# One row of a transposed activation: from four TensorE transposes to a transposing transfer, in a kernel whose instruction order is a table

## The chip, the cores and the metric

The kernel runs on one core of a Trainium2 chip. The metric is the time of one execution on the device in microseconds (us). Before the change the median of three executions was 614.86 us (614.82 to 615.6).

The engines of a core run side by side, each through its own queue in order: PE (TensorE, matrix products), DVE (VectorE), ACT (ScalarE), POOL (GpSimd) and SP (which here only issues transfers). An instruction that waits for a semaphore holds back everything behind it on its engine.

## The reference

One transformer block in float32 on 2048 rows of 512 numbers:

```
h  = x + A(layernorm(x))
h2 = h + B(layernorm(h))
A(x): q, k, v = x @ wqkv, 32 heads of 16; each position attends to 8 positions,
      itself and those 2, 4, ... 14 back; softmax; (attn @ v) @ wo
B(x): (gelu(x @ w_gate) * (x @ w_up)) @ w_down       with an inner width of 1792
```

What matters here is the seam between the two halves: B's products need layernorm(h) transposed, features on the partitions.

## The kernel before, in words

**Tiling.** The 2048 rows are four chunks (c = 0 to 3) of 512, each of four "rows" (j = 0 to 3): tiles of 128 positions on the partitions. Every float32 product is made as three products of rounded operands: a value is cut into a high part (copied on ACT, `split`, L412) and a low part (the rest, subtracted on DVE or POOL, L413), and PE adds high x high, high x low and low x high. So each tile that goes into a product appears as a pair, `hTh` and `hTl` for the transposed h.

**Stages.** Chunk by chunk: project to q, k and v (`project_pair`, with a scheme that shares products between two rows, L764; `project`, L501, for v), attention on DVE (`pk`, `lg`, `pv`), the output product `wo` (L501), then the feed-forward half in 14 steps (`pg`, `pu`, `acc`). Chunks 2 and 3 end together in `joint` and `last_sums`. The stages of different chunks overlap: while chunk 0 crosses the seam, PE still has products of chunk 3's projection to do (`qkc_3_0`, `qkc_3_1`, `qkv_3_2_...`).

**The seam, `tail(c)`, L939.** For each row j of a chunk: PE makes `wo_c_j` (12 products), DVE adds x to it (L968, into `h`), takes statistics (L478, L479), POOL makes the reciprocal deviation (L480, L481), DVE writes the normalised row `xhat_h` (L482). The row is then transposed in one of two ways. `transpose4` (L419): four PE transposes into one PSUM bank (L424), then the high part is copied by ACT and the low part subtracted by DVE from there. `crossed` (L451): ACT copies the row's 32-bit words into planes of 16-bit halves (L436), SP issues a transposing transfer back over the row (L438), ACT weaves the halves together again (L442), and the split follows. The table `CROSS_H` (L63) names the rows of each chunk that are crossed. The first product of the feed-forward half, `pg_0_0`, reads all four rows of `hTh_0`.

```
    def turn(src, flat, tmp, w=D, into=False):

        words = lambda t: t()[:, 0:w].bitcast(U16)
        planes, pairs = "p (h f) -> p h f", "p (f h) -> p h f"
        act(w * 1.65 + 100, lambda: nc.scalar.copy(words(tmp).rearrange(planes, h=2), words(flat).rearrange(pairs, h=2)),
            src, [(tmp, None)])
        plan.add("SP", 1330, lambda: nc.sync.dma_start_transpose(
            words(flat).rearrange("p (k t) -> p k t", t=P), words(tmp)), [(tmp, None)], src, nbytes=800 * w)
        if into:
            return
        act(w * 2.28 + 100, lambda: nc.scalar.copy(words(tmp).rearrange(pairs, h=2), words(flat).rearrange(planes, h=2)),
            src, [(tmp, None)])
...
        a = ring(n, 2, [P, D], name=f"a_{nm}", at=lambda k: slots[k])
        turn(src, flat, a, w)
        split(hi, lo, lambda: a()[:, 0:w].rearrange("p (k t) -> p k t", t=P), [(a, None)], wh, wl, size=w)
```

**Buffers in turn.** The normalised rows `xhat_h` have two buffers and so have the planes `a_h`: row 2 uses those of row 0, and row 3 the `xhat_h` buffer of row 1. A buffer is free again when its last reader is done. For `xhat_h` of a crossed row that is the second ACT copy (L442), for `a_h` the low part's subtraction (L413). The PSUM banks of `wo_0_j` alternate between two as well. The feed-forward weights come in as `fraw_0_f` (768 KB each, L1025); the buffer of `fraw_0_0` held chunk 3's sums `xS_3_1`, which the last products of `qkc_3_1` read.

**The order.** Nothing on the chip chooses an order. The program first lists about 2860 operations with their dependences; then `Plan.schedule` (L305) sorts them by a number each from the table `PLACES` (L64), and the table `SWAPS` (L220) names operations that go to their other engine (ACT or DVE, DVE or POOL). Every engine's queue is the sorted list, restricted to it.

## Time and profile before

| | |
|---|---|
| median of three executions | 614.86 us |
| the profiled execution | 615.18 us, of which span 613.1 us |
| instructions in the profile | 8418 |
| PE busy | 606.3 us (99%), 2692 matmuls and transposes |
| DVE busy | 523.4 us (85%) |
| ACT busy | 472.7 us (77%) |
| POOL busy | 364.3 us (59%) |
| granted TensorE clock | 0.999 |
| TensorE transposes of rows of h (`tp_h`) | 12, three rows of four |
| transposing transfers of rows of h | 13 |

The span reaches from the first to the last instruction; what is over in the execution's own time (2.1 us) lies around it. Matmuls are pipelined: one of 512 columns is listed with 389 ns, but the next one starts 227 to 228 ns later. In the lists below, rows of PE are therefore longer than their cadence.

### The profile page before, as it was taken

To read this page: it belongs to the slowest core of one execution; us is meant where nothing else is said; L and a number is where in the kernel's file an instruction comes from. 1 tells how busy PE (TensorE), PEld (TensorE's weight loads), DVE (VectorE), ACT (ScalarE), POOL (GpSimd) and SP (SyncE) were. 2 spreads that over 40 slices of the span, in tenths; PEclk is the share of its full clock that TensorE was granted. 3 is DMA by queue.
4 is the path that set the end of the run, shared out by engine and by line. 5 is a ranking of instruction groups with operands and counts; after the bars stand their busy time and mean duration, and the time that the engine had idled before them with its cause. 6 is when DMAs were issued, how large, how long until landed. Compare 5 with 4: busy or idle time off the path is not lost.

```text
span 613.1 us, 8418 instructions
## 1 busy us (share of the span) xinstructions
PE 606.3 (99%) x2692; PEld 498.8 (81%) x2692; DVE 523.4 (85%) x644; ACT 472.7 (77%) x822; POOL 364.3 (59%) x349
## 2 busy tenths in 40 slices
PE   8999999999999999999999999999999999999997
PEld 6778888888888888888888888888887888888886
DVE  6989999998999989999999979347977886779933
ACT  5998999748678879999779988768876656658850
POOL 4649898535899847695866944516324535422491
PEclk9999999999999999999999999999999999999999
DMA  8469888887999979999997979987479765557983
GB/s 301 140 231 257 266 238 253 257 276 220 316 333 336 296 239 295 305 284 309 375 353 239 289 227 208 298 267 221 114 246 231 236 215 190 203 190 209 253 259 103
DMA packets 110012, 154.50 MB, mean 252 GB/s; under 512 B 51456, under 2 KB 64512, under 8 KB 109584
## 3 DMA queue, kind: packets, MB, share of 16 engines
q1 hardware_dynamic: 109552, 153.57, 80.7%
q8 instruction: 21, 0.34, 0.2%
q10 hardware_dynamic: 416, 0.39, 0.2%
q14 instruction: 23, 0.19, 0.1%
HBM read 106.43 MB, written 36.23 MB: 233 GB/s over the span
## 4 chain that ended last, share of the span: by engine, by line
PE 95%; DMA 2%; DVE 1%; POOL 1%; issue 0%; ACT 0%; POOLq 0%
PE pg L501 12%; PE pu L501 12%; PE dn L1324 10%; PE pa L1206 8%; PE qkv L501 8%; PE wo L501 7%; PE qka L764 6%; PE pc L1206 5%; PE acc L1006 4%; PE acc L1005 4%; PE acc L1004 4%; PE qkc L764 3%; PE pu L1447 2%; PE pg L1447 2%; PE qkb L764 2%; DMA fraw<-in_wffn_dram 1%
## 5 line engine op out<-in xcount | busy, mean ns | idle before, releaser
L916 POOL TENSOR_TENSOR pv<-pv 128x1024 f32<-128x1024 f32 (+1 forms) x40 | 78.1, 1959 | 6.7 <-DVE pv L911 4.9
L911 DVE TENSOR_TENSOR pv<-vw,qp 128x2048 f32<-128x2048 f32 x32 | 72.2, 2281 | 5.3 <-ACT qp L891 4.4
L869 DVE TENSOR_TENSOR pk<-kw,qp 128x2048 f32<-128x2048 f32 x32 | 72.9, 2280 | 0.5 <-DMA kw<-kv 0.2
L872 DVE TENSOR_REDUCE lg<-pk 128x128 f32<-128x2048 f32 x32 | 72.7, 2279 | 0.1
L501 PE MATMUL pg<-hTh,gu 128*128 128x512 f32 x224 | 59.9, 389 | 0.0
L501 PE MATMUL pu<-hTh,gu 128*128 128x512 f32 x224 | 59.9, 389 | 0.0
L501 PEld LDWEIGHTS pg<-hTh,gu 128*128 128x128 f32 x224 | 42.0, 188 | 8.9 <-ACT hTh L412 0.2
L501 PEld LDWEIGHTS pu<-hTh,gu 128*128 128x128 f32 x224 | 42.0, 188 | 8.7
L1004 PE MATMUL acc<-dnh,gh 128*128 128x512 f32 x112 | 43.7, 390 | 0.0
L1006 PE MATMUL acc<-dnh,gl 128*128 128x512 f32 x112 | 43.6, 390 | 0.0
L1005 PE MATMUL acc<-dnl,gh 128*128 128x512 f32 x112 | 43.6, 389 | 0.0
L1236 ACT COPY jt<-pa 128x512 f32<-128x512 f32 x32 | 18.8, 586 | 25.8 <-PE pa L1206 15.2
L413 POOL TENSOR_TENSOR gu<-fraw,gu 128x512 fp32r<-128x512 f32 x25 | 32.5, 1309 | 7.2 <-ACT gu L412 7.2
L918 POOL TENSOR_TENSOR o<-pv 128x256 f32<-128x256 f32 x27 | 22.9, 854 | 16.8 <-DVE pv L916 11.3
L1206 PE MATMUL pa<-tt,jh 128*128 128x512 f32 x112 | 30.1, 391 | 0.1
L501 PE MATMUL pg<-hTl,gu 128*128 128x512 f32 x112 | 29.9, 389 | 0.0
L501 PE MATMUL pu<-hTl,gu 128*128 128x512 f32 x112 | 29.9, 389 | 0.0
L413 POOL TENSOR_TENSOR gl<-g,gh 128x512 fp32r<-128x512 f32 x21 | 27.2, 1299 | 3.9 <-ACT gh L412 3.9
L1206 PEld LDWEIGHTS pa<-tt,jh 128*128 128x128 f32 x112 | 20.9, 188 | 4.8 <-ACT jt L1236 0.5
L1006 PEld LDWEIGHTS acc<-dnh,gl 128*128 128x128 f32 x112 | 21.0, 188 | 4.5 <-DVE gl L413 0.2
L1005 PEld LDWEIGHTS acc<-dnl,gh 128*128 128x128 f32 x112 | 21.0, 188 | 4.4
L501 PEld LDWEIGHTS pg<-hTl,gu 128*128 128x128 f32 x112 | 21.0, 188 | 4.4
(512 smaller groups left out, 1841.8 us busy)
## 6 DMA issues: line engine op xcount, KB each, us to landing
fraw<-in_wffn_dram SPq DMA_DIRECT2D x47, 768.0 KB, 5.7
kw<-kv SPq DMA_DIRECT2D x16, 704.0 KB, 6.2
vw<-kv SPq DMA_DIRECT2D x16, 704.0 KB, 6.2
gu<-ld SPq DMA_DIRECT2D x19, 512.0 KB, 5.4
kv<-qkvt SPq DMA_DIRECT2D x32, 256.0 KB, 3.3
ld<-gu SPq DMA_DIRECT2D x14, 512.0 KB, 3.9
ws<-sums_kw SPq DMA_DIRECT2D x21, 256.0 KB, 2.3
x<-in_x_dram SPq DMA_DIRECT2D x16, 256.0 KB, 4.8
```

The lines of the kernel that those rows point to most:

```text
L413: sub = lambda eng: eng.tensor_tensor(lo(), src(), hi().bitcast(F32), op=ALU.subtract)
L501: nc.tensor.matmul(acc(), a, b, start=(p == k == 0 and not seeded), stop=(p == n - 1 and k == KD - 1), skip_group_check=seeded)
L764: nc.tensor.matmul(acc(), a(k), b()[:, k], start=first and q == k == 0, stop=q == 2 and k == 1, skip_group_check=not first)
L869: nc.vector.tensor_tensor(pr(), k4, q2.unsqueeze(2).to_broadcast([P, 2, W, QF]), op=ALU.mult)
L872: dve(2195, lambda pr=pr, jj=jj: nc.vector.tensor_reduce(lg()[:, i, jj:jj + 2], pr().rearrange("p j w (h d) -> p j w h d", d=DH), axis=AX. ...
L911: nc.vector.tensor_tensor(pr().rearrange("p j w (h d) -> p j w h d", d=DH), v5, e5, op=ALU.mult)
L916: either(home, 256 * m, lambda eng, pr=pr, m=m: eng.tensor_tensor(pr()[:, :, 0:m], pr()[:, :, 0:m], pr()[:, :, m:2 * m], op=ALU.add), [], ...
L1004: nc.tensor.matmul(a, gh()[:, sl], dh(), start=(i == 0 and not SEED), stop=False, skip_group_check=SEED)
L1005: nc.tensor.matmul(a, gh()[:, sl], dl(), start=False, stop=False, skip_group_check=SEED)
L1006: nc.tensor.matmul(a, gl()[:, sl], dh(), start=False, stop=(i == NF - 1), skip_group_check=SEED)
L1206: nc.tensor.matmul(acc(), a[:, k], b(k), start=first and p == k == 0, stop=p == 2 and k == 1, skip_group_check=not first)
L1324: nc.tensor.matmul(acc(), a[0]()[:, cols], b[0](), start=first and q == 0, stop=last and q == 2, skip_group_check=True)
```

## The change

Row 2 of chunk 0's h is crossed, as rows 0 and 1 are, in place of being transposed by PE. The list of operations grows by two (2858 to 2860): `transpose4` gives one PE operation and a split from PSUM, `crossed` gives two ACT copies, one transfer and a split from SBUF. Both tables are replaced, so operations move on all engines.

```diff
-CROSS_H = ((0, 1), (0, 1, 2, 3), (0, 1, 2, 3), (0, 1, 2))
+CROSS_H = ((0, 1, 2), (0, 1, 2, 3), (0, 1, 2, 3), (0, 1, 2))
 PLACES = (
-    4740, 9385, 0, 825, 1032, 1239, 1446, 1653, 1860, 2067, 2274, 2481, 2688, 2895, 3102, 3309, 3516, 3723, 3930, 4137, 4344, 4551, 4758, 4965, 5172,
...
 SWAPS = (
-    44, 47, 59, 89, 167, 173, 174, 178, 234, 238, 240, 241, 250, 254, 349, 366, 462, 464, 470, 476, 477, 478, 557, 559, 570, 571, 577, 586, 588, 599, 600,
...
+    44, 47, 50, 59, 62, 65, 79, 167, 174, 178, 234, 238, 240, 241, 250, 254, 354, 457, 464, 470, 476, 477, 478, 479, 480, 557, 559, 570, 572, 577, 586,
...
```

What the tables do to the queues is shown at three places. The names carry a running number at their end; `x4` is four instructions alike.

**First place, PE, the end of chunk 3's q and k projection.** `qkc_3_1` is one PSUM bank that is filled twice: first with six products of `wT_3`, which DVE then takes out (L779), then with six of `wh_0` and `wl_0`. `qkc_3_0` is another bank, `tp_o` a transpose of attention output. Before:

```order
L764 MATMUL qkc_3_1_1333<-wT_3_233,xS_3_1_1226 128x512 x4
L764 MATMUL qkc_3_1_1333<-wT_3_233,xSl_3_1_1266 128x512 x2
L424 MATMUL tp_o_0_3_2_1348<-ident_68,o_0_3_1302 128x128 x2
L764 MATMUL qkc_3_0_1185<-wh_0_212,xS_3_0_1118 128x512 x2
L764 MATMUL qkc_3_0_1185<-wl_0_226,xS_3_0_1118 128x512 x2
L764 MATMUL qkc_3_0_1185<-wh_0_212,xS_3_0_1118 128x512 x2
L764 MATMUL qkc_3_1_1333<-wh_0_212,xS_3_1_1226 128x512 x2
L764 MATMUL qkc_3_1_1333<-wl_0_226,xS_3_1_1226 128x512 x2
L764 MATMUL qkc_3_1_1333<-wh_0_212,xS_3_1_1226 128x512 x2
L501 MATMUL wo_0_0_1375<-wo_h_1340,oTh_0_1113 128x512 x4
```

The same stretch of PE's queue now:

```order
L764 MATMUL qkc_3_1_1324<-wT_3_326,xS_3_1_1217 128x512 x4
L764 MATMUL qkc_3_1_1324<-wT_3_326,xSl_3_1_1255 128x512 x2
L424 MATMUL tp_o_0_3_0_1338<-ident_68,o_0_3_1317 128x128 x2
L764 MATMUL qkc_3_1_1324<-wh_0_216,xS_3_1_1217 128x512 x2
L764 MATMUL qkc_3_1_1324<-wl_0_234,xS_3_1_1217 128x512 x2
L764 MATMUL qkc_3_1_1324<-wh_0_216,xS_3_1_1217 128x512 x2
L424 MATMUL tp_o_0_3_2_1358<-ident_68,o_0_3_1317 128x128 x2
L764 MATMUL qkc_3_0_1163<-wh_0_216,xS_3_0_1105 128x512 x2
L764 MATMUL qkc_3_0_1163<-wl_0_234,xS_3_0_1105 128x512 x2
L764 MATMUL qkc_3_0_1163<-wh_0_216,xS_3_0_1105 128x512 x2
L501 MATMUL wo_0_0_1375<-wo_h_1332,oTh_0_1175 128x512 x4
```

The six products of `qkc_3_0` stood between the two fillings of `qkc_3_1` and now stand behind them; two transposes are left between.

**Second place, DVE, from row 0's h to its normalised form.** `dnl_0_0` is the low part of a feed-forward weight, which needs the load `fraw_0_0` and ACT's copy `dnh_0_0`. Before:

```order
L968 TENSOR_TENSOR h_0_1319<-wo_0_0_1375,h_0_1319 128x512
L478 BN_STATS st_h0_0_1408<-h_0_1319 128x6
L479 BN_AGGR mv_h0_0_1414<-st_h0_0_1408 128x2
L779 SCALAR_TENSOR_TENSOR qkvt_3_0_1247<-qkc_3_0_1185,mvx_3_738,qkvt_3_0_1247 128x4x128
L968 TENSOR_TENSOR h_0_1319<-wo_0_1_1396,h_0_1319 128x512
L482 TENSOR_SCALAR xhat_h0_0_1426<-h_0_1319,mv_h0_0_1414,rs_h0_0_1417 128x512
```

And now:

```order
L968 TENSOR_TENSOR h_0_1320<-wo_0_0_1375,h_0_1320 128x512
L478 BN_STATS st_h0_0_1408<-h_0_1320 128x6
L479 BN_AGGR mv_h0_0_1411<-st_h0_0_1408 128x2
L413 TENSOR_TENSOR dnl_0_0_1413<-fraw_0_0_1361,dnh_0_0_1402 128x512
L779 SCALAR_TENSOR_TENSOR qkvt_3_0_1246<-qkc_3_0_1163,mvx_3_741,qkvt_3_0_1246 128x4x128
L482 TENSOR_SCALAR xhat_h0_0_1428<-h_0_1320,mv_h0_0_1411,rs_h0_0_1419 128x512
```

A subtraction that reads a load now stands ahead of row 0's normalised form.

**Third place, PE and ACT, the rest of the seam of chunk 0.** PE from row 3's `wo` to the first feed-forward product, before:

```order
L501 MATMUL wo_0_3_1436<-wo_l_1345,oTh_0_1113 128x512 x4
L501 MATMUL wo_0_3_1436<-wo_h_1340,oTl_0_1224 128x512 x4
L501 MATMUL qkv_3_2_3_1485<-wh_2_272,xTh_3_3_1161 128x512 x4
L501 MATMUL qkv_3_2_2_1498<-wh_2_272,xTh_3_2_1137 128x512 x4
L501 MATMUL qkv_3_2_3_1485<-wl_2_409,xTh_3_3_1161 128x512 x4
L424 MATMUL tp_h_0_2_1522<-ident_68,xhat_h0_2_1510 128x128 x4
L501 MATMUL qkv_3_2_3_1485<-wh_2_272,xTl_3_3_1182 128x512 x4
L501 MATMUL qkv_3_2_2_1498<-wl_2_409,xTh_3_2_1137 128x512 x4
L424 MATMUL tp_h_0_3_1546<-ident_68,xhat_h0_3_1531 128x128 x4
L501 MATMUL qkv_3_2_2_1498<-wh_2_272,xTl_3_2_1172 128x512 x4
L501 MATMUL pg_0_0_1562<-hTh_0_1533,gu_0_0_1447 128x512 x4
```

PE now:

```order
L501 MATMUL wo_0_3_1455<-wo_h_1332,oTh_0_1175 128x512 x4
L501 MATMUL wo_0_3_1455<-wo_l_1335,oTh_0_1175 128x512 x4
L501 MATMUL wo_0_3_1455<-wo_h_1332,oTl_0_1236 128x512 x4
L501 MATMUL qkv_3_2_1_1180<-wh_2_265,xTl_3_1_1023 128x512 x4
L501 MATMUL qkv_3_2_2_1493<-wh_2_265,xTh_3_2_1152 128x512 x4
L501 MATMUL qkv_3_2_2_1493<-wl_2_413,xTh_3_2_1152 128x512 x4
L501 MATMUL qkv_3_2_2_1493<-wh_2_265,xTl_3_2_1170 128x512 x4
L501 MATMUL qkv_3_2_3_1521<-wh_2_265,xTh_3_3_1160 128x512 x4
L424 MATMUL tp_h_0_3_1541<-ident_68,xhat_h0_3_1532 128x128 x4
L501 MATMUL qkv_3_2_3_1521<-wl_2_413,xTh_3_3_1160 128x512 x4
L501 MATMUL qkv_3_2_3_1521<-wh_2_265,xTl_3_3_1173 128x512 x4
L501 MATMUL pg_0_0_1567<-hTh_0_1500,gu_0_0_1400 128x512 x4
```

The four transposes `tp_h_0_2` are gone. From the first `wo_0_0` to `pg_0_0` PE has 76 products in both orders (48 of `wo`, 28 of `qkv_3_2`), and beside them two transposed rows before and one now. ACT's queue over the same seam, now, from row 1's first copy on:

```order
L436 COPY a_h_0_1_1474<-xhat_h0_1_1466 128x1024
L442 COPY a_h_0_0_1439<-xhat_h0_0_1428 128x2x512
L412 CAST hTh_0_1500<-a_h_0_0_1439 128x4x128
L827 ACTIVATE qkvt_3_2_1462<-qkv_3_2_1_1180,mvx_3_741 128x4x128
L436 COPY a_h_0_2_1517<-xhat_h0_2_1502 128x1024
L442 COPY a_h_0_1_1474<-xhat_h0_1_1466 128x2x512
L862 COPY qp_460<-q_1_0_1370 128x256
L412 CAST hTh_0_1500<-a_h_0_1_1474 128x4x128
L412 CAST hTh_0_1500<-tp_h_0_3_1541 128x4x128
L442 COPY a_h_0_2_1517<-xhat_h0_2_1502 128x2x512
L412 CAST hTh_0_1500<-a_h_0_2_1517 128x4x128
```

Before, ACT had L442 of rows 0 and 1 one behind the other and then the four casts of `hTh_0`, rows 2 and 3 of them from PE's banks. Now row 2's first copy stands ahead of row 1's second one, and row 2's own second copy and cast are the last two.

325 rows, old and new, of tables (PLACES, SWAPS) are left out of this document.

## The prediction

> **What bounds the kernel now.** First the page's busy shares, then its chain of waits by engine, then busy time by stretch (stretch; PE with its count, PE's weight loads, DVE, ACT, POOL; clock, transfers).
>
> ```profile
> PE 606.3 (99%) x2692; PEld 498.8 (81%) x2692; DVE 523.4 (85%) x644; ACT 472.7 (77%) x822; POOL 364.3 (59%) x349
> PE 95%; DMA 2%; DVE 1%; POOL 1%; issue 0%; ACT 0%; POOLq 0%
> 20.00:100.00 80.00, 79.90 (x350) 64.56 (x349) 76.58 (x77) 74.55 (x131) 62.59 (x62) 1.00 0.74 221
> 100.00:200.00 100.00, 100.00 (x447) 82.23 (x447) 95.95 (x101) 72.82 (x117) 69.24 (x62) 1.00 0.90 290
> 126.00:146.00 20.00, 20.00 (x93) 16.24 (x92) 16.59 (x28) 11.74 (x18) 6.53 (x11) 1.00 0.76 249
> ```
>
> PE is the bound: it never pauses between 100 and 200 us, where chunk 0 crosses the seam, and the chain that ended last is PE for 95%. So the end moves by two things alone: work taken from PE, and holes opened in PE. DVE, ACT and POOL matter only where PE comes to wait for them. The last row is the seam itself: DVE and ACT have 3.4 and 8.3 us to spare in 20, so it is order and latency, not load, that can open a hole.
>
> **The change part by part.**
>
> *Removed from PE.* From the list of PE in order of time (start, length, what) and, for the cadence, the longest piece of the chain:
>
> ```profile
> 124.54 0.38 PE L424 MATMUL tp_o<-ident,o 128*128 128x128 f32 x2
> 124.67 0.71 PE L764 MATMUL qkc<-wh,xS 128*128 128x512 f32 x2
> 127.53 1.07 PE L501 MATMUL wo<-wo_h,oTh 128*128 128x512 f32 x4
> 142.21 0.60 PE L424 MATMUL tp_h<-ident,xhat_h 128*128 128x128 f32 x4
> 142.56 1.18 PE L501 MATMUL qkv<-wh,xTl 128*128 128x512 f32 x4
> 143.58 1.08 PE L501 MATMUL qkv<-wl,xTh 128*128 128x512 f32 x4
> 145.87 1.09 PE L501 MATMUL pg<-hTh,gu 128*128 128x512 f32 x4
> 560.22 47.85 PE dn L1324 x210
> ```
>
> 47.85 / 210 gives 0.228 us a product. From 142.21 to 143.58 is 1.37 us, and four products in it are 0.91, so four transposes cost 0.46 us. Term: -0.46. If all else stayed hidden, that would be the whole effect.
>
> *Hole A, q and k of chunk 3.* Before, the six products of `qkc_3_0` (1.37 us) ran while DVE took out the first filling of `qkc_3_1`; now only two transposes do, 0.22 us by half of the 0.46. The taking out, by line of the program (count; shortest, median, longest in ns):
>
> ```profile
> L779 DVE SCALAR_TENSOR_TENSOR qkvt<-qkc,mvx,qkvt x12: 646/738/769, 64.6 to 132.1; 128x512 f32<-128x512 f32 x12
> ```
>
> From the start of the last product of the first filling: 0.39 us until it is out of the array (0.389 is the listed length of each), 0.74 on DVE, an estimated 0.1 for the hand-overs (three of 0.02 to 0.05, as between the rows of the seam below), 1.23 in all. Less its own cadence 0.23 and the transposes 0.22: a hole of 0.78. DVE could be busy with something else (one 0.69 us subtraction stands near), which gives 1.5 as the upper bound; 0.7 with the fastest L779. Term: +0.78.
>
> *Hole B, the seam.* DVE, ACT and SP in order of time, and the crossed rows' lengths by tile:
>
> ```profile
> 133.78 0.54 DVE L482 TENSOR_SCALAR xhat_h<-h,mv_h,rs_h 128x512 f32<-128x512 f32 x1
> 142.74 0.55 DVE L482 TENSOR_SCALAR xhat_h<-h,mv_h,rs_h 128x512 f32<-128x512 f32 x1 [1.01 <-ACT a_h L442]
> 134.35 1.05 ACT L436 COPY a_h<-xhat_h 128x1024 uint16<-128x1024 uint16 x1 [2.37 <-DVE xhat_h L482]
> 141.29 1.37 ACT L442 COPY a_h<-xhat_h 128x1024 uint16<-128x1024 uint16 x1 [0.21 <-DMA xhat_h<-a_h]
> L436 ACT COPY a_h<-xhat_h x13: 1034/1046/1053, 134.3 to 423.9; 128x1024 uint16<-128x1024 uint16 x13
> L438 SPq DMA_TRANSPOSE xhat_h<-a_h x13: 1233/1238/1522, 135.4 to 425.0; - x13
> L442 ACT COPY a_h<-xhat_h x13: 1342/1361/1375, 139.7 to 428.7; 128x1024 uint16<-128x1024 uint16 x13
> L412 ACT CAST hTh<-a_h x13: 605/620/628, 143.3 to 436.0; 128x512 fp32r<-128x512 f32 x13
> L413 DVE TENSOR_TENSOR hTl<-a_h,hTh x5: 683/684/694, 144.1 to 436.6; 128x512 fp32r<-128x512 f32 x5
> DMA to landing us min/median/max: 3.0/3.3/5.9
> ```
>
> A crossed row goes through L436 (1.05 us), the transfer (3.0 undisturbed), L442 (1.36) and the cast (0.62). With two buffers of `a_h`, row 2's L436 must wait until row 0's low part is subtracted (0.69), which waits for row 0's cast. So from the end E of row 0's normalised form to `pg_0_0` there now stands one line: row 0 1.05 + 3.04 + 1.36 + 0.62 + 0.69, row 2 1.05 + 3.04 + 1.36 + 0.62, which is 12.83, and ten hand-overs of 0.02 to 0.05, together 0.4: 13.2 us. Before, row 2 had no such leg, and E to `pg_0_0` was 145.87 - 134.32 = 11.6 with PE as the one that came last. Let W be the start of `wo_0_0`, 127.53 before. PE gets from W to `pg_0_0` in 145.87 - 127.53 = 18.34, now less the four transposes: W + 17.88. E was W + 6.79.
>
> E moves, since `dnl_0_0` now stands ahead of it and needs the load `fraw_0_0`. Loads of that tensor in this stretch, by tile, and their issues on SP and ACT's copy that waited for one:
>
> ```profile
> DMA to landing us min/median/max: 5.0/5.8/6.6
> 126.34 0.33 SPq L373 DMA_DIRECT2D fraw<-in_wffn_dram  x1
> 127.72 0.33 SPq L373 DMA_DIRECT2D fraw<-in_wffn_dram  x1
> 131.35 0.62 ACT L412 CAST dnh<-fraw 128x512 fp32r<-128x512 f32 x1 [3.73 <-DMA fraw<-in_wffn_dram]
> ```
>
> The load that reuses the buffer of `xS_3_1` is issued as `qkc_3_1` ends: its last product started one cadence before W, at 127.30, was out at 127.69, and SP issued at 127.72. Now 0.22 of transposes and 1.37 of `qkc_3_0` follow before W, so the issue is at W - 1.4 and the landing, with 5.8, at W + 4.4. ACT casts a part of `gu_0_0` and then `dnh_0_0` (0.62 each, overlapping, 1.15), DVE subtracts (0.69, the next 0.6 after its start), does L779 (0.66 to the next) and then row 0's form (0.55): E = W + 7.4. `pg_0_0` is ready at W + 20.6 and PE is there at W + 17.9: a hole of 2.7, which will show in parts, at `tp_h_0_3` and at `pg_0_0`. The first part comes because row 3's form needs the buffer that row 1's L442 frees, and that copy now stands behind row 2's L436 on ACT: E + 8.0 + 1.4 + 0.6 = W + 17.4 against PE's W + 15.5. Bounds: a landing in 5.0 gives E = W + 6.6 and 1.9; earlier still, DVE's own work for row 0 (0.68, 0.69 and 0.18 behind the first 2.9 of `wo`, then 0.6 + 0.66 + 0.55) ends E no earlier than W + 6.4, which gives 1.7. A landing in 6.6 gives W + 8.2 and 3.5. Term: +2.7.
>
> SP spends 1.24 us on the added issue; behind it stand stores that PE doesn't wait for there. ACT gets 2.4 us more work and DVE a subtraction of equal length (0.69 from PSUM before, 0.68 now): both lie in the spare time of the stretch's row and count only through the line above.
>
> *The rest of the order.* Everything else is moved too, and can't be priced move by move. What the trace has as holes of PE outside the start, and the transfers around the first:
>
> ```profile
> 68.61 0.61 PE L764 MATMUL qkc<-wh,xS 128*128 128x512 f32 x2
> 69.27 0.74 PE L764 MATMUL qka<-wh,xTh 128*128 128x512 f32 x2
> 471.50 0.72 PE L1206 MATMUL pc<-hTh,jh 128*128 128x512 f32 x2 [0.24 <-DVE jt L1228]
> DMA to landing us min/median/max: 2.1/4.1/7.7
> ```
>
> At 69.27 PE starts 0.2 late and goes on slowly, 0.3 in all, and at 471.50 it is some 0.5 late. Both could vanish: -0.3 and -0.5. In the first stretch (20 to 100 us) DVE is busy for 76.58 of 80, so whatever DVE ends there is near PE's need of it; v's banks are emptied by ACT into a buffer that four stores of `kv` must leave first, and those stores land 2.1 to 7.7 us after issue. One such landing at the median 4.1 in place of 2.5 would cost 1.5. I take +0.5 for this stretch (-0.3 to +1.5), nearer to no change since the same buffers were met before, and +0.2 for the end (-0.5 to +1.5).
>
> *Sum:* -0.46 + 0.78 + 2.7 + 0.5 + 0.2 = +3.7 us. The profiled execution took 615.18 (span 613.1 and 2.1 around it), 0.32 over the median of 614.86. I add to the median: **618.6 us**, in a profile of that kind a span near 616.8.
>
> **A rule of the Trainium skill.** The trace's row stands above: 3.0 us at least from issue to landing of a transposing transfer, and 1.05 + 1.36 us of copies around it, against 0.46 on PE. The Trainium skill's page "VectorE: DVE Perf Modes", section "The three transpose paths", gives 1309 ns for a transposing transfer of 128x128 in two-byte words against 390 ns for TensorE's, and its section "Rules for kernel authors" says to use TensorE where a PSUM destination will do. It speaks against the change in direction. By 1.31 in place of 3.04 twice, the line of hole B would shrink by 3.5 us and the hole close; the sum would then be an estimated +1.0. The trace differs and decides.
>
> **The rivals.**
>
> 1. *The order hides row 2* (not slower). If row 0's form were as early as W + 4.7, the line of 13.2 would end as PE arrives; hole A remains if DVE's L779 isn't quicker than any seen. For it speaks only that the load was the last to be met in 3.73 us by ACT and that DVE had 3.4 us spare; against it, the W + 6.4 from DVE's own rows. With B gone, A at 0.7 and the first stretch at -0.3: 614.9. With A gone too: 614.4. It decides if E is before W + 5.5 (hole under 0.9). Chance 0.13, of which 0.03 below 613.6.
> 2. *Late transfers make it larger.* The load takes 6.6 us as one of the two did (B 3.5), the first stretch costs 1.5 and the end 1.5: -0.46 + 0.8 + 3.5 + 1.5 + 1.5 = +6.8, 621.7. For it speaks the stretch's transfers at 0.76 to 0.95 of their engines; against it, that all three must be late. From 620.5 on; chance 0.19.
> 3. *A pause slows PE afterwards.* Rows of the start, and the longest pause that PE makes later:
>
> ```profile
> 2.00:4.50 2.50, 2.50 (x14) 2.50 (x13) 0.00 (x0) 0.44 (x1) 0.08 (x1) 1.00 0.68 203
> 4.50:7.00 2.50, 1.33 (x12) 1.09 (x10) 1.16 (x5) 1.04 (x4) 0.00 (x0) 1.00 1.05 392
> 7.03 0.75 PE L564 MATMUL tp_x<-ident,xhat_x 128*128 128x128 f32 x4 [1.20 <-ACT xhat_x L557]
> ```
>
> A transpose takes 2.50/14 = 0.18 us before 4.5 us and 1.33/12 = 0.11 after, while the clock's column says 1.00 for both: PE starts at some 0.6 of its pace and warms up within 4.5 us. The four transposes behind the pause of 1.20 us at 7.03 are listed with 0.75, those at 142.21 with 0.60, so that pause cost 0.15 at most; the trace has no longer one. If hole B came as one pause of 2.7 and PE then ran at 0.6 for some 3 us, that costs 3 x 0.4 = 1.2 to 1.7 more (0.5 of the pace): about 620.2. Against it: B is expected in two parts, about 1.9 at `tp_h_0_3` and the rest at `pg_0_0`, with products between. Chance 0.06.
>
> The Trainium skill's page "TensorE: Matmul & The Clock Gate", section "Part 1: The HAM clock gate (the "warmup" mystery)", says that the clock halves after an idle window of about 3.4 us and comes back after as long a busy one. By that rule neither part of B is long enough, and nothing is added; the trace's 1.20 us agrees as far as it goes, and no run here shows a longer one.
>
> **How the numbers follow.** About 0.2%, 1.2 us, is what a measurement of this kernel can tell from no change. The forecast, both holes with B between 1.7 and 3.5 and the smaller terms near their values, spans 616.1 to 620.5, with 0.62. Rival 1 has 0.13: 0.10 within 1.2 us, 0.03 below. Rival 2 has 0.19, rival 3 0.06. So faster is 0.03, no change 0.10, slower 0.62 + 0.19 + 0.06 = 0.87. The low end, 616.6, is the forecast with B at its 1.7 and the first stretch and the end at -0.3 and 0 (-0.46 + 0.78 + 1.7 - 0.3 = +1.7); below it lie rival 1 and a little of the forecast. The high end, 622.0, takes in rivals 2 and 3 at their values and leaves out what goes beyond.
>
> **What would show it.** In the changed kernel's profile: (1) four products' time less on PE for transposes, eight `tp_h` instead of twelve and fourteen transposing transfers; (2) PE idle about 0.8 ahead of the second filling's L764 near 126 us, ended by DVE's L779; (3) DVE idle ahead of L413 `dnl`, ended by ACT's cast and that by the load, row 0's L482 ending 7.4 after `wo_0_0` starts (6.8 before); PE idle ahead of a `tp_h` at L424, ended by DVE's L482, and ahead of `pg` at L501, ended by ACT's L412, 2.7 together; (4) by stretch, 3.5 us less of PE than its length between 120 and 155, and under 1 us in all later. The forecast is wrong if PE is never idle through the seam (row 0 early, rival 1), if the load lands before W + 3 and B comes all the same (then the line, not the load, was mispriced), or if the holes lie in other stretches (the two terms of the rest of the order).

## The result, and the profile after

The changed kernel took 620.45 us (median of 4 executions, 620.1 to 622.48), the kernel before 614.84 (median of 4, 614.18 to 615.6): a ratio of 1.0102 with a 95% interval of 1.0089 to 1.0115, so about 5.6 us slower. The prediction was 618.6 in 616.6 to 622.0, slower with 0.87.

The page of the changed kernel (its profiled execution took 620.11 us) has these rows of busy shares and of the chain of waits:

```profile
PE 607.2 (98%) x2688; PEld 499.4 (81%) x2688; DVE 525.4 (85%) x654; ACT 469.5 (76%) x821; POOL 350.7 (57%) x338
PE 84%; DMA 7%; DVE 4%; ACT 2%; issue 1%; SPq 1%; DVEq 0%; ACTq 0%
```

PE does about as much as before, but it is now only 84% of the chain that ended last, and transfers are 7%. Where PE waits, by the waits of PE (engine and line, what it waited for, us in total, times, longest), and by stretch (columns as in the prediction):

```profile
PE tp_h L424 <- DVE xhat_h L482: 1.9, 1, 1.9
PE qkv L501 <- ACT qkvt L827: 1.8, 2, 0.9
PE pg L501 <- ACT hTh L412: 0.7, 1, 0.7
PE qkc L764 <- DVE qkvt L779: 0.6, 1, 0.6
PE qka L764 <- ACT qkvt L774: 0.3, 1, 0.3
60.00:80.00 20.00, 19.12 (x85) 15.50 (x84) 19.48 (x21) 17.73 (x35) 16.93 (x17) 1.00 0.93 278
80.00:100.00 20.00, 19.72 (x86) 15.48 (x85) 19.44 (x16) 18.14 (x31) 17.90 (x16) 1.00 0.79 211
120.00:140.00 20.00, 19.37 (x87) 15.77 (x86) 16.47 (x23) 10.96 (x19) 8.78 (x11) 1.00 0.79 271
140.00:160.00 20.00, 16.44 (x72) 12.73 (x71) 16.61 (x19) 16.64 (x25) 8.57 (x11) 1.00 0.78 219
```

The pauses named in the prediction are there: ahead of L764 (hole A), and ahead of `tp_h` and `pg` (hole B). There are three more: two ahead of L501 `qkv`, ended by ACT's L827, one near 71 us and one in the seam, and a small one ahead of L764 `qka`, ended by ACT's L774, at 84.62 us. The seam's stretch, 140 to 160 us, is short of 3.56 us of PE.

The list of PE in order of time gives the sizes:

```profile
125.47 0.38 PE L424 MATMUL tp_o<-ident,o 128*128 128x128 f32 x2
126.47 0.73 PE L764 MATMUL qkc<-wh,xS 128*128 128x512 f32 x2 [0.63 <-DVE qkvt L779]
129.57 1.07 PE L501 MATMUL wo<-wo_h,oTh 128*128 128x512 f32 x4
145.17 1.20 PE L501 MATMUL qkv<-wh,xTh 128*128 128x512 f32 x4 [0.93 <-ACT qkvt L827]
148.26 0.66 PE L424 MATMUL tp_h<-ident,xhat_h 128*128 128x128 f32 x4 [1.89 <-DVE xhat_h L482]
151.50 1.19 PE L501 MATMUL pg<-hTh,gu 128*128 128x512 f32 x4 [0.75 <-ACT hTh L412]
```

Three marks divide the 5.2 us by which the span grew (613.1 to 618.3). `wo_0_0` starts at 129.57 instead of 127.53, 2.04 later. From there to `pg_0_0` it is now 21.93 instead of 18.34, so `pg_0_0` starts 5.63 later. The end is 5.2 later, so 0.43 comes back behind the seam. Of the 2.04, hole A is 126.47 - 125.47 less the two transposes' 0.23, that is 0.77; the other 1.27 belong to the first stretch. They are a balance: counted along PE's list, its 200th instruction starts 0.6 earlier than before (small pauses between 21 and 24 us are gone), its 400th 1.0 later (the pauses at 70.88 and 84.62 have come). Of the seam's growth, PE has 0.46 less to do, so the hole is 21.93 - 17.88 = 4.05. The three pauses there, from the start of one product to the start of the next less the cadence, come to 4.06.

The seam on ACT, DVE and SP:

```profile
135.54 0.55 DVE L482 TENSOR_SCALAR xhat_h<-h,mv_h,rs_h 128x512 f32<-128x512 f32 x1
137.48 0.62 ACT L412 CAST dnh<-fraw 128x512 fp32r<-128x512 f32 x1 [3.14 <-DMA fraw<-in_wffn_dram]
138.00 1.04 ACT L436 COPY a_h<-xhat_h 128x1024 uint16<-128x1024 uint16 x1
128.16 0.33 SPq L373 DMA_DIRECT2D fraw<-in_wffn_dram  x1
129.77 0.33 SPq L373 DMA_DIRECT2D fraw<-in_wffn_dram  x1
139.07 2.09 SPq L438 DMA_TRANSPOSE xhat_h<-a_h  x1
DMA to landing us min/median/max: 4.5/6.1/7.7
```

Row 0's form is done at 136.09, which is `wo_0_0` + 6.5. But its first copy on ACT, L436, starts at 138.00. Ahead of it in ACT's queue stands the copy of the **second** weight load, `dnh_0_1`, and that waited 3.14 us for the load issued at 129.77, which landed 7.7 us later. From the start of L436 to `pg_0_0` it is 13.5 us; the prediction's line for that way was 13.2. DVE did not wait ahead of `dnl_0_0`: the first load, issued at 128.16, had landed after 4.5 us.

### The profile page after: what moved, and what is told of

It reads as the page before. It is cut to its first block, busy times and chain, and to the rows that moved or that the text cites. A ratio compares the mean times of both kernels' runs of the same rounds, so it can differ in the third digit from the quotient of the medians.

```text
span 618.3 us, 8414 instructions
## 1 busy us (share of the span) xinstructions
PE 607.2 (98%) x2688; PEld 499.4 (81%) x2688; DVE 525.4 (85%) x654; ACT 469.5 (76%) x821; POOL 350.7 (57%) x338
## 4 chain that ended last, share of the span: by engine, by line
PE 84%; DMA 7%; DVE 4%; ACT 2%; issue 1%; SPq 1%; DVEq 0%; ACTq 0%
PE pg L501 12%; PE pu L501 12%; PE dn L1324 10%; PE pa L1206 8%; PE wo L501 5%; PE qkv L501 5%; PE pc L1206 5%; PE acc L1004 4%; PE acc L1006 4%; PE acc L1005 4%; PE qka L764 4%; PE pu L1447 2%; PE pg L1447 2%; PE qkc L764 2%; DMA fraw<-in_wffn_dram 2%; DMA kv<-qkvt 2%
## 5 line engine op out<-in xcount | busy, mean ns | idle before, releaser
L916 POOL TENSOR_TENSOR pv<-pv 128x1024 f32<-128x1024 f32 (+1 forms) x41 | 79.4, 1940 | 16.1 <-DVE pv L916 9.8
L501 PE MATMUL pg<-hTh,gu 128*128 128x512 f32 x224 | 60.0, 390 | 0.7 <-ACT hTh L412 0.7
L501 PE MATMUL pu<-hTh,gu 128*128 128x512 f32 x224 | 59.9, 389 | 0.0
L501 PEld LDWEIGHTS pg<-hTh,gu 128*128 128x128 f32 x224 | 42.0, 188 | 9.8 <-ACT hTh L412 1.2
L501 PEld LDWEIGHTS pu<-hTh,gu 128*128 128x128 f32 x224 | 42.0, 188 | 8.7
L413 POOL TENSOR_TENSOR gl<-g,gh 128x512 fp32r<-128x512 f32 x22 | 29.5, 1341 | 5.9 <-ACT gh L412 5.9
L501 PE MATMUL pg<-hTl,gu 128*128 128x512 f32 x112 | 29.9, 389 | 0.0
L501 PE MATMUL pu<-hTl,gu 128*128 128x512 f32 x112 | 29.9, 389 | 0.0
L413 POOL TENSOR_TENSOR gu<-fraw,gu 128x512 fp32r<-128x512 f32 x19 | 25.5, 1349 | 7.2 <-ACT gu L412 7.1
L918 POOL TENSOR_TENSOR o<-pv 128x256 f32<-128x256 f32 x22 | 17.2, 784 | 17.7 <-DVE pv L916 8.7
L412 ACT CAST gu<-fraw 128x512 fp32r<-128x512 f32 x28 | 17.1, 616 | 10.4 <-DMA fraw<-in_wffn_dram 9.1
L1061 DVE TENSOR_TENSOR g<-pu,g 128x512 f32<-128x512 f32 x28 | 19.1, 681 | 6.5 <-PE pu L501 3.7
```

Source lines behind the costliest of these rows:

```text
L413: sub = lambda eng: eng.tensor_tensor(lo(), src(), hi().bitcast(F32), op=ALU.subtract)
L501: nc.tensor.matmul(acc(), a, b, start=(p == k == 0 and not seeded), stop=(p == n - 1 and k == KD - 1), skip_group_check=seeded)
L916: either(home, 256 * m, lambda eng, pr=pr, m=m: eng.tensor_tensor(pr()[:, :, 0:m], pr()[:, :, 0:m], pr()[:, :, m:2 * m], op=ALU.add), [], ...
```

## The experiments

Two theories stood against each other after this reading. **The line**: the seam's hole is what row 2 adds behind row 0, as predicted. **The late load**: rows 0 and 1 start late because loads and stores that land late hold up ACT's queue, and would do so without row 2. All comparisons are with the kernel before, on the same chip and in the same set.

### Which stretch costs what

**first_only** and **seam_only** take the order of one kernel up to 116 us and that of the other behind it: the key by which the operations are sorted becomes a pair, as below, and each operation keeps the engine that goes with it.

```diff
-PLACES = (
-    4740, 9385, 0, 825, 1032, 1239, 1446, 1653, 1860, 2067, 2274, 2481, 2688, 2895, 3102, 3309, 3516, 3723, 3930, 4137, 4344, 4551, 4758, 4965, 5172,
...
+first_only key:  (0, changed[n]) if changed[n] < 116000 else (1, before[n])
+seam_only key:   (0, before[n]) if before[n] < 116000 else (1, changed[n])
```

> The changed order up to 116 us, the order of before (row 2 through PE) behind it. If the two pauses of PE at 70.88 and 84.62 us in the changed profile belong to the new order of the first stretch and have nothing to do with the seam, they stay, and the time is about 1.3 us over before: 616.1 (615.6 to 616.6). If they were that execution's landings and not the order, or if the seam causes them, the time is that of before, 614.9.

Measured: 616.01 us, ratio 1.0016 (1.0005 to 1.0027), so 1.0 us. The pauses stay in its list of PE:

```profile
70.66 2.11 PE L501 MATMUL qkv<-wh,xTh 128*128 128x512 f32 x8 [0.61 <-ACT qkvt L827]
84.62 0.72 PE L764 MATMUL qka<-wh,xS 128*128 128x512 f32 x2 [0.52 <-ACT qkvt L774]
```

They belong to the new order of the first stretch and, less what that order saves between 21 and 24 us, cost about 1 us, whatever the seam does.

> The order of before up to 116 us, the changed one behind it. If the account adds up, the first stretch's 1.3 goes and the rest stays: 0.8 from the hole ahead of the second filling, some 4 from the seam, less 0.46 and less 0.4 at the end: 619.0 (618.4 to 619.6). If the two stretches hang together, 620.4 or 614.9.

Measured: 619.25 us, ratio 1.0075 (1.0057 to 1.0094), 4.6 us. The two parts add up to the whole within their intervals.

### Hole A alone

**move_only** is the kernel before with `qkc_3_0`'s products, and the load that waits for their buffer, moved behind the second filling.

```diff
+MOVED = {497: 125682, 871: 125683}
-            o.start = start
+            o.start = MOVED.get(o.n, start)
```

> The kernel before, row 2 through PE; only the six products of qkc_3_0 go behind the second filling of qkc_3_1 (and with them the load fraw_0_1, whose buffer they free). The prediction's hole A alone: PE idle 0.7 to 0.8 at L764 ahead of the second filling, nothing else: 615.6 (615.3 to 615.9). If the move also makes the second weight load and the stores behind it land late and these hold row 0's first copy (L436) on ACT, as in the changed kernel, the seam gets a hole too: 616.3 (615.9 to 617.3), with the wait of ACT for the load in the trace. No hole: 614.8.

Measured: 616.02 us, ratio 1.0015 (1.0005 to 1.0025), 0.9 us. The hole is there, and from `wo_0_0` to `pg_0_0` nothing is:

```profile
126.80 0.73 PE L764 MATMUL qkc<-wh,xS 128*128 128x512 f32 x2 [0.84 <-DVE qkvt L779]
134.16 0.62 ACT L412 CAST dnh<-fraw 128x512 fp32r<-128x512 f32 x1 [4.93 <-DMA fraw<-in_wffn_dram]
136.47 1.05 ACT L436 COPY a_h<-xhat_h 128x1024 uint16<-128x1024 uint16 x1 [1.69 <-DVE xhat_h L482]
148.07 1.10 PE L501 MATMUL pg<-hTh,gu 128*128 128x512 f32 x4
```

Hole A is confirmed in place and, roughly, in size: 0.84 of listed pause, or 0.99 if reckoned as the 0.77 above (126.80 - 125.58 less 0.23), where 0.78 was forecast. The second half of the expectation did not come: here the load that the copy ahead of L436 needs lands in time, and L436 waits for DVE, not for that copy. But the two loads also keep their old order. SP issues `fraw_0_1` first, at 129.84, and it lands after 4.3 us; `fraw_0_0` follows at 130.23. In the changed kernel `fraw_0_1` is the second and takes 7.7, and ACT's copies stand in another order too. So the move alone doesn't make the seam late. Which of the other two does, the order of the loads or that of ACT's copies, was not separated.

### The late load and row 2, each alone and both

**late_load** puts the copy of the second load behind row 0's first copy and its subtraction behind row 1's deviation.

```diff
+MOVED = {878: 134500, 879: 135760}
-            o.start = start
+            o.start = MOVED.get(o.n, start)
```

> The changed kernel, but ACT's copy of the second weight load (dnh_0_1) stands behind row 0's first copy (L436), and POOL's subtraction of it behind row 1's deviation. Theory of the late load: ACT stood 1.9 us for that load with row 0's form ready, so row 0 starts 1.9 earlier, until the next wait (ACT's L827 ahead of row 1's first copy, for a store that lands at 138.5) takes over: about 1.4 us less, 619.0 (618.5 to 619.4), and the holes of the seam come to the 2.7 of the prediction. Rival: the first transposing transfer was itself held by the stores that landed at 139.1, as the chain of waits has it; then it starts no earlier, and the time stays at 620.4. The prediction's theory (row 0's form is what comes late, because of the first load) also gives 620.4.

**row2_pe** keeps the changed order and gives row 2 back to PE.

```diff
-CROSS_H = ((0, 1, 2), (0, 1, 2, 3), (0, 1, 2, 3), (0, 1, 2))
+CROSS_H = ((0, 1), (0, 1, 2, 3), (0, 1, 2, 3), (0, 1, 2))
+PLACES = PLACES[:708] + PLACES[713:722] + (141926, 142200, 143600) + PLACES[722:]
+SWAPS = tuple(n if n < 708 else n - 5 if n < 722 else n - 2 for n in SWAPS if not 708 <= n < 713)
```

> The changed order, with row 2 of chunk 0 turned by four PE transposes again. The prediction's theory: the hole of the seam is row 2's line, so it closes, at +0.46 on PE: 616.7 to 617.3. Theory of the late load: rows 0, 1 and 3 are late all the same, row 2's line takes only what stands behind row 1, so the time falls by 0.8 alone: 619.6 (619.2 to 620.0).

**both** does the two together, with the load's two numbers shifted by the list's two fewer operations.

```diff
+MOVED = {876: 134500, 877: 135760}
```

> The changed order with row 2 through PE and the second load's copy and subtraction out of the way: late_load and row2_pe together. If the two causes stand one behind the other in the seam, their gains add: 0.6 to 1.4 from the load, 0.5 to 0.8 from the row: 618.4 (617.8 to 618.9), the rest being the first stretch (1.0), hole A (0.8) and what is left of the pause ahead of row 3's transposes. If each only uncovers the other's wait, it stays at 619.4.

**after_again** is the changed kernel in another set, for comparison.

> The changed kernel as it is, beside the three others of this set and the kernel before on the same chip. 620.4 (619.9 to 620.9). If the pauses of PE at the seam (0.9, 1.9 and 0.8 us within 8 us) let the granted clock fall in some executions, as it did in the execution of seam_only that was profiled, then some executions show a mean granted clock of 0.998 or less, which the kernel before does not; if they don't, all show 0.999 and more.

| | median us | ratio to before | interval |
|---|---|---|---|
| after_again | 619.98 | 1.0081 | 1.0066 to 1.0096 |
| late_load | 619.36 | 1.0080 | 1.0063 to 1.0097 |
| row2_pe | 619.50 | 1.0075 | 1.0058 to 1.0092 |
| both | 618.78 | 1.0065 | 1.0053 to 1.0078 |

The kernels were not all in one set, so the ratios are to be compared. No single pair of these is clear of noise: each interval is 1.5 to 2.1 us wide, and the changed kernel itself came to 5.6 us over before in one set and 5.0 in the other. So the traces have to decide, with one execution of each. In them the seam is measured from the start of `wo_0_0` to that of `pg_0_0`, less what PE itself needs there (17.88, or 18.34 with row 2 on PE):

| | `wo_0_0` | `pg_0_0` | way, us | hole, us |
|---|---|---|---|---|
| the changed kernel | 129.57 | 151.50 | 21.93 | 4.05 |
| late_load | 129.75 | 151.04 | 21.29 | 3.41 |
| row2_pe | 129.15 | 149.93 | 20.78 | 2.44 |
| both | 129.65 | 149.77 | 20.12 | 1.78 |

The load's copy out of the way takes 0.64 off the hole, row 2 on PE takes 1.61 off it, and both together take 2.27: in the traces the gains add, and row 2 is the larger. In late_load, ACT and SP:

```profile
136.31 1.05 ACT L436 COPY a_h<-xhat_h 128x1024 uint16<-128x1024 uint16 x1 [1.80 <-DVE xhat_h L482]
137.38 1.23 SPq L438 DMA_TRANSPOSE xhat_h<-a_h  x1
139.66 0.69 ACT L827 ACTIVATE qkvt<-qkv,mvx 128x512 f32<-128x512 f32 x1 [1.23 <-DMA kv<-qkvt]
142.02 1.36 ACT L442 COPY a_h<-xhat_h 128x1024 uint16<-128x1024 uint16 x1 [0.61 <-DMA xhat_h<-a_h]
DMA to landing us min/median/max: 3.1/3.1/4.6
```

Row 0's first copy starts 1.7 earlier, as the late load has it. But the transposing transfer then takes 4.6 in place of the changed kernel's 3.4, and L442 starts at 142.02, half a microsecond earlier than in the changed kernel. The stores of `kv` were still landing then (the copy behind them waited until 139.66); that they are the reason is read from the times, and no run leaves them out. So both the theory and its rival were half right. The load held the row, and once it didn't, its transposing transfer did. The profiled execution of late_load is the slowest of its six (621.68 us), by pauses behind the seam: from `pg_0_0` to the end of the span it takes 468.9, where the changed kernel takes 466.8.

In row2_pe PE waited 0.66 ahead of `qkv` and 1.48 ahead of `tp_h`, and at `pg` 0.2 alone was lost. The prediction's line would have it 617.3 or less; it is 619.5. So row 2's line is not all that makes this seam late in this order: 2.44 of the hole's 4.05 stay without it. The pause ahead of `tp_h` is there in row2_pe (first two lines) and in both (third line):

```profile
144.48 1.19 PE L501 MATMUL qkv<-wh,xTh 128*128 128x512 f32 x4 [0.66 <-ACT qkvt L827]
147.58 0.66 PE L424 MATMUL tp_h<-ident,xhat_h 128*128 128x128 f32 x4 [1.48 <-DVE hTl L413]
147.43 0.66 PE L424 MATMUL tp_h<-ident,xhat_h 128*128 128x128 f32 x4 [1.47 <-DVE hTl L413]
```

Not all of this pause is lateness. The L413 that ends it is row 2's own subtraction: `transpose4` puts rows 2 and 3 of chunk 0 into the same PSUM bank, so row 3's transposes must wait until row 2 has been read out of it. Row 3's normalised form was done 0.6 us before that in both kernels. So some 0.6 of what stays without the crossed row 2 is row 2 again, by way of the bank.

Both edits together give 1.0 us by the ratios of after_again and both (618.78 measured, inside the expected 617.8 to 618.9), and 1.8 by the traces. What is left, 4.0 over before, is the first stretch (1.0), hole A (0.9), the seam's remaining 1.8 and some 0.3 that is unaccounted for.

### Row 2 in the old order

**row2_only** is the kernel before with nothing but row 2 crossed.

```diff
-CROSS_H = ((0, 1), (0, 1, 2, 3), (0, 1, 2, 3), (0, 1, 2))
+CROSS_H = ((0, 1, 2), (0, 1, 2, 3), (0, 1, 2, 3), (0, 1, 2))
+PLACES = PLACES[:708] + (139240, 139250, 143700, 143710, 143750) + PLACES[708:717] + PLACES[720:]
+SWAPS = tuple(n if n < 708 else n + 5 if n < 717 else n + 2 for n in SWAPS) + (712,)
+MOVED = {683: 137625, 684: 139235}
```

> The kernel before with nothing but row 2 crossed: its five operations put where the two casts and the subtraction of the transposed row stood, row 0's cast and subtraction right behind its second copy so that the planes come free. The prediction's line alone: row 0's form ends at 134.3, plus 13.2 is 147.5, PE is there at 145.4, so a hole of 2.1, less 0.46: 616.4 (616.0 to 616.9). If the copies of row 1, that stand between those of rows 0 and 2 on ACT, add to it (1.36 for L442, 0.6 for each cast), the hole is 3.6: 618.0 (617.4 to 618.6). If the row is hidden: 614.3.

Measured: 618.83 us, ratio 1.0061 (1.0042 to 1.0080). Two lines of PE's list and four of ACT's:

```profile
145.52 0.66 PE L424 MATMUL tp_h<-ident,xhat_h 128*128 128x128 f32 x4 [1.34 <-DVE xhat_h L482]
149.26 1.20 PE L501 MATMUL pg<-hTh,gu 128*128 128x512 f32 x4 [2.16 <-ACT hTh L412]
138.61 1.26 ACT L827 ACTIVATE qkvt<-qkv,mvx 128x512 f32<-128x512 f32 x2
139.76 1.35 ACT L442 COPY a_h<-xhat_h 128x1024 uint16<-128x1024 uint16 x1
146.69 0.62 ACT L412 CAST gu<-fraw 128x512 fp32r<-128x512 f32 x1
147.21 1.35 ACT L442 COPY a_h<-xhat_h 128x1024 uint16<-128x1024 uint16 x1
```

Here the line does what the prediction said of it, and more: 3.5 us of pause against the 2.1 of the line alone. The number is near the expectation's second one (3.6), but not for its reason. Row 1's second copy runs while row 2's transfer is still under way, and delays nothing. What lengthens the line is other work on ACT: the transfer of row 0 had landed at 138.52, and its L442 started 1.2 later behind two L827; that of row 2 had landed at 146.66, and its L442 started 0.55 later behind the copy of a weight. So crossing row 2 has a price of its own of about 3 us in the old order (a hole of 3.8, from 127.57 to 149.26 less 17.88, and 0.46 less on PE). In the new order the hole is 4.05 with it and 2.44 without: the two causes lie in part one over the other in the seam.

**row2_own** gives row 2 its own buffers in that kernel, **own_buffers** does it in the changed order, with late_load's edit and five more places (the first line below; row2_own has only the two others).

```diff
+MOVED = {878: 134500, 879: 135760, 524: 137030, 708: 139806, 709: 139807, 683: 140331, 684: 141806}
...
+        a = T("o1", [P, D], name=f"a_{nm}") if nm == "h_0_2" else ring(n, 2, [P, D], name=f"a_{nm}", at=lambda k: slots[k])
+        dst = T("o0", [P, D], name=f"xhat_{nm}") if nm == "h0_2" else ring("xhat", 2, [P, D], name=f"xhat_{nm}")
```

> The row2_only version (the order of before, row 2 crossed), with buffers of its own for row 2 as in own_buffers. If the buffers in turn make the line, the hole shrinks from 3.8 towards what row 2 needs from its own form on (1.05 + 3.04 + 1.36 + 0.62, with its form at 141.7: ready at 148, PE there at 145.4: 2.6), so 1.2 less: 616.6 with a full clock, 617.6 as a median. If ACT's queue decides (row 1's second copy and cast, row 3's cast), 0.5 less: 617.3 with a full clock, 618.3 as a median. No change: 618.8. The pause then comes in one piece ahead of pg, near 3 us.

> The late_load version, and row 2 has buffers of its own for its normalised form and its planes (those of the attention output, free there), so that it waits for neither row 0's second copy nor its subtraction; row 2's first copy stands ahead of row 0's cast on ACT, and ACT's L827 behind row 1's first copy. If the two buffers in turn are what makes row 2's line long, the holes of the seam come to 1.7 in place of 3.6: 618.2 (617.6 to 618.7). If the buffers don't matter and the landings decide, it stays where late_load was: 619.4.

row2_own took 617.95 us, ratio 1.0055 (1.0041 to 1.0069), and has one pause in place of two:

```profile
148.12 2.07 PE L501 MATMUL pg<-hTh,gu 128*128 128x512 f32 x4 [2.58 <-ACT hTh L412]
146.00:147.00 1.00, 0.00 (x0) 0.00 (x0) 0.38 (x1) 1.00 (x2) 1.00 (x2) 1.00 0.59 219
147.00:148.00 1.00, 0.00 (x0) 0.00 (x0) 0.00 (x0) 0.97 (x3) 0.76 (x1) 0.79 0.57 98
150.00:151.00 1.00, 1.00 (x4) 0.81 (x3) 0.99 (x1) 0.00 (x0) 0.00 (x0) 0.50 0.09 37
151.00:152.00 1.00, 1.00 (x6) 0.81 (x5) 0.98 (x1) 0.96 (x2) 0.00 (x0) 1.00 0.00 0
```

The buffers were worth 0.9 of the 3.5 us of pause, between the two expectations (1.2 and 0.5), but of this gain the time loses a part again: PE's granted clock is 0.50 from 147.6 to 151.0, and the first four products of `pg` take 2.07 us instead of 1.2. own_buffers took 619.55 (1.0057 to 1.0087), no better than late_load. In its profiled execution, the slowest of its six (621.14), the first load took 6.5 us to land, and DVE waited for it just as the prediction had it, ahead of row 0's form:

```profile
135.52 0.69 DVE L413 TENSOR_TENSOR dnl<-fraw,dnh 128x512 fp32r<-128x512 f32 x1 [1.81 <-ACT dnh L412]
```

Row 0's form was then done at `wo_0_0` + 8.2, which is what the prediction gave for a landing in 6.6. So of two loads either can be the one that holds the seam.

### The clock

seam_only's profiled execution shows the same as row2_own's, over a longer time:

```profile
143.88:145.00 1.12, 1.12 (x4) 0.67 (x4) 0.87 (x3) 1.00 (x2) 0.13 (x1) 1.00 0.05 17
145.00:146.00 1.00, 0.08 (x1) 0.00 (x0) 0.00 (x0) 1.00 (x2) 0.66 (x2) 1.00 0.00 0
146.00:146.50 0.50, 0.00 (x0) 0.00 (x0) 0.14 (x1) 0.50 (x3) 0.00 (x0) 0.62 0.45 90
149.00:150.00 1.00, 1.00 (x3) 0.73 (x3) 1.00 (x3) 0.97 (x2) 0.69 (x1) 0.50 0.00 0
152.75:153.00 0.25, 0.25 (x3) 0.17 (x2) 0.25 (x1) 0.25 (x1) 0.06 (x1) 0.61 0.59 172
```

A mean of 0.62 over 146.0 to 146.5 puts the fall at 146.12, the 0.61 puts the return at 152.95: 6.83 us at half speed. In row2_own it is 147.58 to 151.0, 3.42. The mean granted clock of each execution tells how often it happens (0.997 and less against 0.999 and more):

| kernel | pauses of PE in the seam, us | least PE in 3.42 us, us | executions at 0.997 or less |
|---|---|---|---|
| before | none | 3.42 | 0 of 49 |
| first_only, move_only, old_with_new_start | none | 2.6 or more | 0 of 35 |
| own_buffers | 0.5, 1.2, 0.5, 0.8 | 2.2 | 0 of 6 |
| both | 1.5 | 1.9 | 0 of 5 |
| row2_pe | 0.7, 1.5 | 1.6 | 0 of 6 |
| late_load | 0.3, 1.9, 0.8 | 1.3 | 3 of 6 |
| row2_only | 1.3, 2.2 | 1.3 | 3 of 6 |
| seam_only | 1.2, 1.9 | 1.2 | 3 of 6 |
| the changed kernel, both sets | 0.9, 1.9, 0.8 | 1.2 | 7 of 10 |
| row2_own | 2.6 | 0.8 | 4 of 5 |

The third column is how long PE was busy, by its list in the profiled execution, in the emptiest stretch of 3.42 us around the seam (120 to 160 us). It parts the kernels that fell (1.3 or less) from those that never did (1.6 or more). The longest single pause parts them too (1.9 or more against 1.5 or less), but the fall in seam_only speaks for the sum of neighbouring pauses: it came 1.04 us into the second pause, after a first one of 1.16, and row2_pe and both have a pause of 1.5 without a fall. A stretch that empty need not bring the fall: the changed kernel's profiled execution had 1.2 us of PE between 144.84 and 148.26 and kept its clock. What decides between the executions of one kernel, these runs don't show.

A stretch of row2_pe, whose clock never fell, as the profile shows it:

```profile
144.20:147.60 3.40, 1.65 (x9) 1.19 (x9) 2.37 (x6) 2.98 (x5) 0.79 (x2) 1.00 0.58 216
```

The changed kernel's three executions with a full clock have a median of 619.8, its seven others 620.8; row2_only's 617.8 and 620.0.

**fill** tests it: seven products whose result nobody reads, in the pause ahead of row 3's transposes.

```diff
-            for k in range(n):
-                nc.tensor.transpose(tp()[:, k * P:(k + 1) * P], srcs(k), ident())
+            for k in range(-7 if nm == "h_0_3" else 0, n):
+                nc.tensor.matmul(tp(), oT[0][0]()[:, 0, 0], wo_h()[:, 0], start=True, stop=True) if k < 0 else nc.tensor.transpose(tp()[:, k * P:(k + 1) * P], srcs(k), ident())
```

> The changed kernel, and ahead of row 3's transposes PE does seven products more whose result nobody reads (0.23 us each, 1.6 us, into the bank that the transposes then overwrite), in the pause of 1.9 us before them. If it is PE's idling that lets the clock fall, no execution shows a mean granted clock under 0.999, and the time is that of the changed kernel's executions with a full clock, 619.4 to 620.1, without those near 622: 619.7. If the clock falls for another reason, about half still show 0.998 or less. If PE wasn't free there, the products cost their 1.6: 621.5.

Measured: 619.61 us, ratio 1.0080 (1.0067 to 1.0094). Four executions, 619.07 to 620.14, all have 0.999 or 1.0, while 7 of the 10 without the products had 0.997 or less; on the same chip and in the same set row2_own fell in 4 of 5. One more, the profiled one, took 3099 us, with PE some five times slower from its first to its last instruction and the other engines as busy as ever. It is left out of the comparison, and since it is the only one of fill that was traced, no trace shows the seam of the other four. PE's idling lets the clock fall, then, though four executions are few.

### A version meant to beat both

**old_with_new_start** takes the changed order up to 40 us, where it has no pauses, and the order of before behind it.

```diff
+old_with_new_start key:  (0, changed[n]) if changed[n] < 40000 else (1, before[n])
```

> The changed order up to 40 us, the order of before behind it, row 2 through PE. The order of before has four small pauses of PE between 21 and 24 us (0.6 in all by the cadence), the changed one has none there. If that holds, it is 0.5 faster than before and so than both: 614.4 against 614.9. If landings later take it back: no change.

Measured: 615.01 us, ratio 1.0004 (0.9995 to 1.0012): no change. None of these versions beats the kernel before.

## Why the prediction was right, and where it was not

The sign, the range and the two holes' places were right. The sum came to +3.7 and the profiled span grew by 5.2. That the total lay inside the range is partly luck: the wait that was forecast at the start of hole B did not come, and another one that was not in the sum came in its place. By its terms:

- **Removed from PE, -0.46.** Not measured by itself. The list of instructions has 8 transposes of rows of h in place of 12 and 14 transposing transfers in place of 13. It agrees that PE's way through the seam less its pauses is 17.9 in the changed kernel and 18.3 in the kernel before.
- **Hole A, +0.78.** 0.77 in the changed kernel, 0.99 by the same reckoning and +0.9 us (0.3 to 1.5) in move_only. Right, by the steps that the prediction gave.
- **Hole B, +2.7 (1.7 to 3.5).** 4.05, outside its bounds. The line from row 0's first copy to `pg_0_0` was right (13.5 against 13.2), and it ran through row 0 and row 2 in the order given. The start of it was the step that failed: "So from the end E of row 0's normalised form to `pg_0_0` there now stands one line" lets ACT take row 0 up as E comes. The load that was priced was issued where the prediction had it (W - 1.4), but landed earlier than I took it (4.5, not 5.8), so DVE did not wait for it and E was W + 6.5, not 7.4; of the third sign, DVE's wait ahead of `dnl` did not come. The other load, which reuses the buffer of `xS_3_0`, was not priced. I had moved `qkc_3_0` for hole A, and not asked what its end releases. That load's issue went from ahead of the other's to behind it, it landed 7.7 after its issue, and its copy stands in ACT's queue ahead of row 0's L436. E came 0.9 earlier, and ACT started 1.9 later than E.
- **The cause behind hole B.** The prediction gave it to row 2's line. row2_only shows that line at work in the old order (3.5 us of pause), lengthened there by ACT's other work. In the new order the traces give it the largest single part: with row 2 on PE the hole is 2.44 in place of 4.05, and the way through the seam 1.15 shorter, since PE then does the row's 0.46 again. The second load's copy ahead of L436 is 0.64 of the hole, and 1.78 stays without either. By the ratios of after_again and row2_pe row 2 adds 0.4 us, which is not clear of their intervals (1.8 and 2.1 us wide); the sizes rest on one traced execution of each kernel.
- **The first stretch, +0.5 (-0.3 to +1.5).** 1.27 in the profile, 1.0 by first_only. In the bounds, and in part by the mechanism named: near 70 us ACT's L827 waits 0.29 for a store of `kv`, of the 0.88 that PE then waits. The pause of 0.6 or so that went between 21 and 24 us was not in the term.
- **The end, +0.2.** -0.43, near the lower bound of -0.5, but not by the change. From `pg_0_0` to the end the kernel before takes 467.2 in its trace and the changed one 466.8, while move_only and old_with_new_start, with the old order there, take 466.7 and 466.5. So the half microsecond, the pause near 471.5 that the prediction listed, comes and goes with the execution.

Of the rivals, the first (no hole) did not come. The second, late transfers, is what the time resembles (621.7 against 620.45), and of its three conditions the first stretch came near (1.27 of its 1.5), hole B was made larger by a late load, but another load than the one it named, and the 1.5 at the end did not come. The third, a pause that slows PE, had 0.06 and came in seven of ten executions, at about 1 us each where 1.2 to 1.7 were forecast. My reason against it, that the two parts of hole B lie apart with products between them, did not hold. The Trainium skill's page "TensorE: Matmul & The Clock Gate", section "Part 1: The HAM clock gate (the "warmup" mystery)", speaks of an idle window of about 3.4 us that is free-running and does not reset when a kernel starts. The trace agrees on the length (3.42 and twice 3.42 at half speed), but PE was not idle throughout the 3.42 us before the fall: it was busy for 1.2 of them in seam_only (the products from 143.88 to 145.08) and for 1.4 in row2_own. I had read the rule as one about a single pause.

## What to carry to other kernels

When a step moves, list what its end releases: buffers, the loads waiting for them, and the queues in which those loads' readers stand ahead of others. A pause of PE has to be added up with its neighbours. In these runs the clock fell in the kernels where PE was busy for some 40% or less of a stretch of 3.4 us (in 20 of their 33 executions), and never in those where it was always busy for some 48% or more. An edit that merges or lengthens pauses then pays for it a second time. Replacing 0.46 us of PE by a chain of 6 us pays only where the chain has 6 us of slack, and the slack is read from the end of the row's own data to the first reader, over every queue between them.

## What was not expected

- Of two loads of 768 KB, issued 1.6 us apart in the changed kernel, the first took 4.5 us from issue to landing and the second 7.7. A transposing transfer that took 3.0 to 3.4 there took 4.6 when it was issued 1.7 earlier (late_load).
- The granted clock falls to 0.50 for 3.42 or 6.83 us, in about half of the executions of one and the same kernel. Seven products that compute nothing, put in the pause, kept it up.
- One execution of fill ran PE at a fifth of its speed throughout. Its mean granted clock is given as 1.0, but its page has no row of the granted clock, as the other pages have, so that number shows nothing; nothing in these runs says why PE was slow.
